# Unused tiles between the pools of a two-MLP kernel: moving operands begin 64 to 256 bytes off the weights' place in a 512-byte row

## The chip, the cores and the metric

The kernel runs on one core of one Trainium2 chip. The metric is device time in microseconds (us) of one execution; less is better. Engines are named as the profile names them: PE is TensorE's matmuls, PEld its weight loads, DVE is VectorE, ACT is ScalarE, POOL is GpSimd, SP the engine that issues the transfers.

## What is computed

Causal retention over 4 batches of 576 tokens with 8 heads of 64, then two MLPs over the 2304 x 512 result, all in float32:

```python
ret = scores * Dmat[None, :, :, :]          # Dmat: gamma_h ** (i - j) for i >= j, else 0
attn = np.matmul(ret, v)
x = attn.transpose(0, 2, 1, 3).reshape(2304, 512)
h = np.maximum(x @ moe_w_in, 0.0)           # 512 -> 2048
x = (h * h) @ moe_w_out                     # 2048 -> 512
h = x @ moe2_w_in
g = h * np.clip(h + 3.0, 0.0, 6.0) / 6.0
return g @ moe2_w_out
```

## The kernel before

**Stages.** The 2304 tokens go through retention and the first MLP in five blocks of 512 or 384 tokens, `BLOCKS`, whose x lies in turn in two tiles, "xa" and "xb". Within a block the loop goes over 16 slices of 128 hidden units. For each, `h_part` (line 612) multiplies a slice of w_in with x (12 matmuls at line 624), ScalarE and VectorE turn the result into g, and `a_part` (line 646) multiplies a slice of w_out with g (12 matmuls at line 661) into four accumulators. Retention of later chunks of 128 tokens stands between these slices, with many matmuls of 64 columns (lines 409 to 497); the first four chunks come ahead of all (lines 277 to 329). While the blocks run, the weights of the second MLP are split and stored for later. The second MLP then runs over three supers of 768 tokens with seven products where a 2 x 2 block product has eight: 112 groups of matmuls with x at line 1185, then as many with the split activations at line 1239.

**Operands.** A float32 number is kept as a high part and a low rest, both of type float32r; each product is made of three matmuls (high with high, high with low, low with high). A matmul has 128 x 128 weights, 512 bytes in each partition, loaded ahead of it, and a moving operand of 512 or 384 columns. Every matmul has its own load. The order of all work is written out by hand; for the second MLP a small clock in the program, `now`, says where the other engines' work is put into the order.

**Where tiles lie.** Tiles come out of pools, and the pools form two stacks in each partition's memory: "left" ones grow up from its bottom, "right" ones down from its top. On the left lie small tiles (`cpool`, `tmpp`), then `gpool` (two g tiles), `xapool` (x of a block of 512), `whi` (weights of slices 8 to 15). On the right lie an unused tile of 320 bytes, "align" (line 107), `upool`, `wlo` (weights of slices 0 to 7), `xbpool` (x of a block of 384) and `apool` (retention). For the second MLP the right stack down to `upool` is taken away (line 1016) and `p1a` put there: its operands of x, `xop` (line 792), six of seven slots of the weights' ring (`ring_load`, line 938), and `spl`, the split activations (`a_cast`, line 1105). When the first MLP is over, the left stack goes as well (line 1040), and `p1c` takes its place with the seventh ring slot and the activations. Sizes are nearly all multiples of 512 bytes. With the 320 bytes of "align" all weights and all moving operands of both MLPs begin 160 bytes into a 512-byte row of the partition's memory, on both stacks.

```python
    pool(ctx, "align", 1, side="right").tile([P, 80], F32, tag="align", name="align")
    upool = pool(ctx, "upool", 1, side="right")
    wlo = pool(right, "wlo", 1, side="right")
    xbpool = pool(right, "xbpool", 1, side="right")
```

## Time and profile before

| | |
|---|---|
| median of 3 runs | 809.81 us (809.74 to 810.19) |
| the profiled execution | 810.17 us |
| its span, first to last instruction | 808.4 us |
| PE busy | 798.3 us, 99% |
| PEld busy | 743.8 us, 92% |
| DVE busy | 604.0 us, 75% |
| ACT busy | 397.0 us, 49% |
| POOL busy | 172.8 us, 21% |
| share of 16 transfer engines' time, queue 1 | 74.5% |
| mean granted clock of TensorE | 0.999 |

The span is the time from the first to the last instruction of one profiled execution; the 1.8 us between it and that execution's own time lie around it. An engine's busy time counts its records' time, a matmul's from its start to a modelled end, so that records of matmuls that follow each other overlap; the step from start to start is read from stretches of the chain, their length divided by their count.

### The profile page before, as it was taken

The page shows a single profiled execution, that of the slowest core. Times are in us where ns is not written, and L with a number is a line of the kernel's source. Part 1 is how long each engine was busy: PE and PEld are TensorE (multiplying, and loading weights), DVE is VectorE, ACT ScalarE, POOL GpSimd, SP SyncE. Part 2 cuts the span into 40 slices and gives each one's busy share as a digit, 9 for nine tenths or more (in the row PEclk, how much of TensorE's full clock was granted, in tenths as well). Part 3 has the DMA queues.
Part 4 walks back from the last instruction along what each step waited for, and adds up shares of the span by engine and source line. Part 5 has one row for each costly group of instructions (what it writes and reads, how often), then busy time and mean ns, then how long its engine had stood idle before and what let it go on. Part 6 is the DMA issues. An engine that isn't in the chain of part 4 may idle for free.

```text
span 808.4 us, 15632 instructions
## 1 busy us (share of the span) xinstructions
PE 798.3 (99%) x5876; PEld 743.8 (92%) x5876; DVE 604.0 (75%) x1106; ACT 397.0 (49%) x736; POOL 172.8 (21%) x163
## 2 busy tenths in 40 slices
PE   8999999999999999999999999999999999999997
PEld 7788889999888899998888999999999999999997
DVE  5989887878755577865557876989677987678764
ACT  1697745444443444444445543666234664335552
POOL 4512230211011011100000056500165300355300
PEclk9999999999999999999999999999999999999999
DMA  9956626777746478766458887979987979977785
GB/s 331 348 191 242 223 92 202 230 220 223 215 145 200 122 246 225 214 175 190 122 162 257 260 295 247 342 269 284 272 257 261 346 253 283 278 258 261 261 235 142
DMA packets 181899, 189.59 MB, mean 235 GB/s; under 512 B 60608, under 2 KB 135488, under 8 KB 181824
## 3 DMA queue, kind: packets, MB, share of 16 engines
q1 hardware_dynamic: 181824, 188.60, 74.5%
q8 instruction: 46, 0.75, 0.4%
q14 instruction: 29, 0.24, 0.1%
HBM read 149.76 MB, written 38.80 MB: 233 GB/s over the span
## 4 chain that ended last, share of the span: by engine, by line
PE 96%; DMA 1%; POOL 1%; issue 0%; SPq 0%; DVE 0%; ACT 0%; DVEq 0%; POOLq 0%
PE acc L661 25%; PE h L624 24%; PE z L1185 22%; PE z L1239 21%; PE at L497 2%; DMA kv<-kv_dram 1%; POOL w L176 0%; PE alone L497 0%; PE sc L409 0%; PE sc L277 0%; PE o L293 0%; POOL raw L141 0%; PE o L460 0%; PE sc L420 0%; DMA out_dram<-t 0%
## 5 line engine op out<-in xcount | busy, mean ns | idle before, releaser
L661 PE MATMUL acc<-g,w 128*128 128x512 f32 (+1 forms) x960 | 212.9, 370 | 0.7 <-ACT g L637 0.4
L624 PE MATMUL h<-x,w 128*128 128x512 f32 (+2 forms) x972 | 210.6, 365 | 0.0
L661 PEld LDWEIGHTS acc<-g,w 128*128 128x128 f32 x960 | 173.8, 188 | 24.9 <-ACT g L637 0.8
L624 PEld LDWEIGHTS h<-x,w 128*128 128x128 f32 x972 | 175.7, 188 | 22.5 <-ACT w L169 0.3
L1185 PE MATMUL z<-xop,ring 128*128 128x384 f32 x1008 | 175.2, 334 | 0.0
L1239 PE MATMUL z<-spl,ring 128*128 128x384 f32 x1008 | 175.2, 334 | 0.0
L1185 PEld LDWEIGHTS z<-xop,ring 128*128 128x128 f32 x1008 | 174.8, 188 | 0.1
L1239 PEld LDWEIGHTS z<-spl,ring 128*128 128x128 f32 x1008 | 174.8, 188 | 0.0
L1100 POOL TENSOR_TENSOR aop<-aop,aop 128x384 f32<-128x384 f32 x96 | 107.5, 1130 | 296.7 <-DVE aop L1097 293.0
L1114 DVE TENSOR_TENSOR spl<-aop,spl 128x384 fp32r<-128x384 f32 x168 | 98.0, 610 | 22.8 <-ACT spl L1110 22.2
L1110 ACT ACTIVATE spl<-aop 128x384 fp32r<-128x384 f32 x168 | 86.0, 523 | 54.7 <-PE z L1239 51.0
L633 ACT ACTIVATE r<-h 128x512 f32<-128x512 f32 (+1 forms) x80 | 44.4, 554 | 112.8 <-PE h L624 112.8
L1094 ACT ACTIVATE aop<-held,small 128x384 f32<-128x384 f32 x72 | 44.4, 617 | 108.3 <-DVE held L1060 107.8
L635 DVE TENSOR_TENSOR r<-r,h 128x512 f32<-128x512 f32 (+1 forms) x80 | 50.5, 631 | 52.7 <-ACT r L633 51.9
L1060 DVE TENSOR_TENSOR held<-z,held 128x384 f32<-128x384 f32 x120 | 66.4, 554 | 26.3 <-PE z L1185 24.1
L637 ACT ACTIVATE g<-r 128x512 fp32r<-128x512 f32 (+1 forms) x80 | 47.2, 590 | 63.3 <-DVE r L635 63.3
L643 DVE TENSOR_TENSOR g<-r,g 128x512 fp32r<-128x512 f32 (+1 forms) x80 | 53.3, 667 | 20.9 <-ACT g L637 18.5
L1097 DVE SCALAR_TENSOR_TENSOR aop<-aop,held 128x384 f32<-128x384 f32 x72 | 49.9, 694 | 17.8 <-ACT aop L1094 16.1
L394 POOL TENSOR_TENSOR qs<-qs,con 128x512 f32<-128x512 f32 x11 | 15.0, 1363 | 134.8 <-DMA qs<-qk_dram 123.0
L751 ACT ACTIVATE uhi<-seven 128x896 fp32r<-128x896 f32 x32 | 30.6, 955 | 23.2 <-DVE seven L741 13.5
L756 DVE TENSOR_TENSOR seven<-seven,uhi 128x896 fp32r<-128x896 f32 x32 | 34.9, 1090 | 7.7 <-ACT uhi L751 7.2
L176 POOL TENSOR_TENSOR w<-wt,w 128x512 fp32r<-128x512 f32 x17 | 22.9, 1347 | 60.2 <-ACT w L169 58.8
(113 smaller groups left out, 628.5 us busy)
## 6 DMA issues: line engine op xcount, KB each, us to landing
ring<-w_out_hl SPq DMA_DIRECT2D x84, 512.0 KB, 4.9
ring<-w_in_hl SPq DMA_DIRECT2D x72, 512.0 KB, 4.8
raw<-w_dram SPq DMA_DIRECT2D x32, 512.0 KB, 7.0
uraw<-w_dram SPq DMA_DIRECT2D x64, 256.0 KB, 3.3
q<-qk_dram SPq DMA_DIRECT2D x17, 512.0 KB, 5.4
w_in_hl<-uhi SPq DMA_DIRECT2D x16, 448.0 KB, 3.6
w_in_hl<-seven SPq DMA_DIRECT2D x16, 448.0 KB, 4.6
w_out_hl<-uhi SPq DMA_DIRECT2D x16, 448.0 KB, 3.2
```

What stands on the lines that cost most here:

```text
L624: nc.tensor.matmul(hp[:, ts], w[:, wi, c * P : (c + 1) * P], x[:, xi, c, ts], start=k == 0, stop=k == 3 * NC - 1,)
L635: nc.vector.tensor_tensor(r, r, hp[:, :nb], ALU.mult)
L637: nc.scalar.activation(g[:, 0, :nb], r, AF.Copy)
L643: nc.vector.tensor_tensor(g[:, 1, :nb], r, g[:, 0, :nb].bitcast(F32), ALU.subtract)
L661: nc.tensor.matmul(acc[d][:, :nb], wt, g[:, gi, :nb], start=first, stop=stop)
L1060: fn(*a)
L1097: stt(f32(q, j), f32(q, j), 6.0, h, ALU.min, ALU.mult)
L1100: nc.gpsimd.tensor_tensor(f32(o, j), f32(a, j), f32(b, j), op)
L1110: act(t[:, 0, :], f32(q, k), AF.Copy)
L1114: tt(t[:, 1, :], f32(q, k), t[:, 0, :].bitcast(F32), ALU.subtract)
L1185: nc.tensor.matmul(bank[q], w[:, wi, u * P : (u + 1) * P], x[:, u, xi, :], start=k == 0 and q not in (2, 4, 3), stop=k == 5, skip_group_ch ...
L1239: nc.tensor.matmul(z[A_BANKS[q][n]][:, :HALF], w[:, k % 2, wi, P * n : P * (n + 1)], sp[:, g, :], start=k == 0 and m == 0 and q not in (2, ...
```

## The change

Between the pools, tiles are allocated that nothing reads or writes, by a new helper `shift`. On the left: 128 bytes below `gpool`, 128 more below `xapool`, 256 more below `whi`, 512 in all. On the right: the 320 bytes of "align" stay, now through the helper, and 256 bytes stand between `wlo` and `xbpool`. In `p1a` a tile of 64 bytes stands between the operands of x and the ring, and another between the ring and what follows it. Built, the places of the operands in a 512-byte row are these:

| matmuls | moving operand | weights |
|---|---|---|
| line 624, h<-x,w | x: 160 before, 416 now | 160, 160 |
| line 661, acc<-g,w | g: 160 before, 288 now | 160, 160 |
| line 1185, z<-xop,ring | xop: 160 before, 32 now | ring: 160 before, 96 now; slot 6: 160, 160 |
| line 1239, z<-spl,ring | spl: 160, 160 | the same ring |

The instructions and their order are those of before on every engine. Of the waits one stands elsewhere: on POOL, the second of the first four operations of line 1100 waits for a count of ScalarE that the third of them waited for before.

```diff
+    def shift(stack, name, size, side):
+
+        pool(stack, name, 1, side=side).tile([P, size // 4], F32, tag=name, name=name)
+
+    shift(left, "shift_g", 128, "left")
     gpool = pool(left, "gpool", 2, side="left")
+    shift(left, "shift_xa", 128, "left")
     xapool = pool(left, "xapool", 1, side="left")
+    shift(left, "shift_whi", 256, "left")
     whi = pool(left, "whi", 1, side="left")
-
-    pool(ctx, "align", 1, side="right").tile([P, 80], F32, tag="align", name="align")
+    shift(ctx, "align", 320, "right")
     upool = pool(ctx, "upool", 1, side="right")
     wlo = pool(right, "wlo", 1, side="right")
+    shift(right, "shift_xb", 256, "right")
     xbpool = pool(right, "xbpool", 1, side="right")
...
             for st in x_first:
                 do(st[0])
+            p1a.tile([P, 16], F32, tag="shift_ring", name="shift_ring")
...
     p1c = pool(ctx, "p1c", 1, side="left")
+    p1a.tile([P, 16], F32, tag="shift_spl", name="shift_spl")
```

## Rows read from the trace of the kernel before

**Rows 1.** The page, part 1: busy us (share of span) x instructions.
```profile
PE 798.3 (99%) x5876; PEld 743.8 (92%) x5876; DVE 604.0 (75%) x1106; ACT 397.0 (49%) x736; POOL 172.8 (21%) x163
```
**Rows 2.** The page, part 4: the chain's shares by engine.
```profile
PE 96%; DMA 1%; POOL 1%; issue 0%; SPq 0%; DVE 0%; ACT 0%; DVEq 0%; POOLq 0%
```
**Rows 3.** Waits of PE: us in total, times, longest us.
```profile
PE sc L277 <- DVE q L265: 1.0, 1, 1.0
PE unread L852 <- POOL early L846: 1.0, 1, 1.0
...
PE acc L661 <- ACT g L637: 0.4, 1, 0.4
PE acc L661 <- POOL w L176: 0.3, 1, 0.3
```
**Rows 4.** The chain in the first MLP: start us, us, what.
```profile
33.49 2.72 PE h L624 x12
36.21 2.72 PE acc L661 x12
...
126.07 2.08 PE acc L661 x12
128.15 2.08 PE h L624 x12
```
**Rows 5.** The chain in the second MLP.
```profile
453.33 58.26 PE z L1185 x336
511.60 58.24 PE z L1239 x336
569.84 58.24 PE z L1185 x336
628.08 58.24 PE z L1239 x336
686.32 58.24 PE z L1185 x336
744.55 56.17 PE z L1239 x324
800.73 0.02 issue
```
**Rows 6.** Busy time in stretches: engines' us (x), granted clock, transfer share, GB/s.
```profile
core 0: us, PE busy (x) PEld busy (x) DVE busy (x) ACT busy (x) POOL busy (x), PEclk, DMA share, GB/s
126.07:138.69 12.62, 12.62 (x173) 12.30 (x173) 9.40 (x22) 5.74 (x11) 0.10 (x1) 1.00 0.68 213
453.33:511.59 58.26, 58.26 (x338) 58.26 (x337) 44.54 (x77) 23.50 (x46) 29.37 (x28) 1.00 0.85 280
511.60:569.80 58.20, 58.20 (x337) 58.20 (x337) 50.17 (x96) 34.58 (x72) 6.38 (x4) 1.00 0.90 296
628.10:686.30 58.20, 58.20 (x337) 58.20 (x337) 49.54 (x95) 34.48 (x71) 6.38 (x4) 1.00 0.92 297
```
**Rows 7.** PE's groups by shape: xcount | busy us, mean ns | idle before.
```profile
L1185 PE MATMUL z<-xop,ring 128*128 128x384 f32 x1008 | 175.2, 334 | 0.0
L1239 PE MATMUL z<-spl,ring 128*128 128x384 f32 x1008 | 175.2, 334 | 0.0
L661 PE MATMUL acc<-g,w 128*128 128x512 f32 x576 | 140.3, 392 | 0.7 <-ACT g L637 0.4 <-POOL w L176 0.3
L624 PE MATMUL h<-x,w 128*128 128x512 f32 x564 | 135.8, 390 | 0.0
L661 PE MATMUL acc<-g,w 128*128 128x384 f32 x384 | 72.7, 337 | 0.0
L624 PE MATMUL h<-x,w 128*128 128x384 f32 x384 | 71.8, 334 | 0.0
...
L624 PE MATMUL h<-x,w 128*128 128x256 f32 x24 | 3.1, 286 | 0.0
```
**Rows 8.** POOL's first operations of line 1100 in the timeline.
```profile
463.13 4.38 POOL L1100 TENSOR_TENSOR aop<-aop,aop 128x384 f32<-128x384 f32 x4 [112.54 <-DVE aop L1097]
```
**Rows 9.** Line 303: one group in PE's timeline; durations min/median/max of all.
```profile
15.41 1.16 PE L303 MATMUL o<-q,states 128*128 128x128 f32 x8
...
L303 PE MATMUL o<-q,states x24: 275/275/377, 15.4 to 22.8; 128*128 128x128 f32 x24
```
**Rows 10.** PEld's groups by shape: weight loads of 128 and 64 columns.
```profile
L1185 PEld LDWEIGHTS z<-xop,ring 128*128 128x128 f32 x1008 | 174.8, 188 | 0.1
...
L497 PEld LDWEIGHTS alone<-p,v 64*64 64x64 f32 x176 | 6.0, 135 | 0.0
```

## The prediction

> **What bounds the kernel now.** I read the page's first part, then the chain that ended last, then TensorE's groups with their shapes, and last single stretches of the chain and of engine time. The first part says that TensorE is the bound: 798.3 of 808.4 us busy, VectorE next with 604.0 [rows 1]. The chain says that nothing else matters: 96% of the span is TensorE, the transfer named next has 1% [rows 2]. Its waits are a few, the longest 1.0 us, all in the start or of that size [rows 3]. So a matmul's step, the time from one start to the next, times the number of matmuls is the kernel.

> The step can be read from stretches of the chain in which TensorE does one thing. Twelve matmuls of 512 columns take 2.72 us, 226.7 ns each; twelve of 384 take 2.08 us, 173.3 ns [rows 4]. In the second MLP 336 of 384 columns take 58.26 or 58.24 us, 173.4 and 173.3 ns [rows 5]. [...] Every matmul thus costs its columns and **32 more, 13.3 ns**, whatever its length and whichever of the four kinds it is. There are 564 + 384 + 24 of the kind h<-x,w, 576 + 384 of acc<-g,w, 1008 of z<-xop,ring and 1008 of z<-spl,ring [rows 7], 3948 in all. Their excess is 3948 x 13.3 = 52.6 us, 6.5% of the span, and that is all this change can get at.

> **The change, part by part.** It adds tiles that nobody writes or reads. No instruction is added, removed or moved on any engine, no transfer changes its size or its pieces; what remains is where tiles lie. I cost four parts.

> The waits. One differs: on POOL the first subtraction of line 1100 waits for a ScalarE count that the second one waited for before. POOL had stood idle 112.54 us before these operations, for VectorE [rows 8], and the ScalarE count lies in the first MLP, long over. Cost 0, and the cover is that idle time; without it the worst would be one operation of about 1.1 us (4.38 us for four) on an engine that no part of the chain between 453.33 and 800.73 us goes through [rows 5, 8].

> VectorE, ScalarE and POOL operations on moved tiles. Each goes over the same elements at another place. They have room: in the second MLP VectorE is busy 50.17 of 58.20 us, ScalarE 34.58 [rows 6]. If each VectorE operation there became a tenth longer, VectorE would still fit (55.2 us). Cost 0.

> Transfers into and out of moved tiles. The ring's pieces land 64 bytes off their former place. In the second MLP the transfer engines are at 0.85 to 0.92 of their time [rows 6], so this is the tightest cover; TensorE would begin to wait if the transfers there got some 9% slower (1/0.92). Nothing in their size or number changes, and I put 0.

> TensorE's own reads, the only term that may be large. In the kernel before, each moving operand of the four kinds begins at the same place of a 512-byte row as its weights, so **the trace shows no step at another distance** between them; the cost has to be bounded. The bound below is the whole excess: 0 columns more instead of 32 gives -52.6 us. The nearest row with a smaller excess is line 303, weights of the same 128 columns, where eight short matmuls take 1.16 us with a last one of 377 ns [rows 9]: (1.16 - 0.377)/7 = 111.9 ns a step. Those steps are paced by the weight loads. A load of 128 columns takes 188 ns and one of 64 takes 135 [rows 10], so 64 columns more are 53 ns, a column is 0.83 ns, and 128 are 106 ns; what is left over is 5.9 ns. If the large matmuls fell to 5.9 ns, they would gain 13.3 - 5.9 = 7.4 ns each, 29.2 us. The bound above is as open: should moving operand and weights stand best as they are, and each load cost the stream as much again, it is +13.3 ns a matmul, +52.6 us.

> Between these ends I take **0**, for two reasons from the rows. First, the two streams do not keep step. Weights are read at 0.83 ns a column [rows 10], the moving operand at 0.417 ns (2.4 per ns). While one 512-byte row of weights is read, the moving operand runs through two rows of its own, so it passes every place of a row twice, and a shift of 64, 128 or 256 bytes changes when the two meet, not how often. Second, the step does not heed other readers: it is the same to 0.1 ns between a stretch with VectorE at 44.54, ScalarE at 23.50 and POOL at 29.37 us busy and one with 50.17, 34.58 and 6.38, with transfers at 0.85 and 0.90 [rows 5, 6]. Those engines go through rows at all places. If meeting at a place cost TensorE a cycle, the steps would scatter with them.

> [...]

> **The sum** is 0 on the profiled execution, which took 810.17 us for a span of 808.4. That is 0.36 above the median of the runs shown, 809.81, so I forecast 809.8; the likeliest case alone lies within 809.0 and 810.6.

> **The rivals.**

> Faster: the excess is the two reads in each other's way, and it is there because they share their place. For it: the excess is the same in all four kinds and at 256, 384 and 512 columns, and in all of them the distance is 0, just the case that the change ends. A cost that comes once for each weight load and not with the columns is what a collision with that load would look like. Against it: the two rates above, and that the slow steps of line 303 also have distance 0 with an excess of only 5.9 ns. Time: 809.8 - 29.2 = 780.6 if all four kinds fall to 5.9 ns; the first MLP alone has 1932 matmuls, 14.3 us, so 795.5, and the second 2016, 14.9 us, so 794.9. One kind's shift may help and another's not, since they are 256, 128 and 64. The far edge is 757.2.

> [...]

> Slower: distance 0 is the good case. The moving operand runs at twice the weights' pace, so from one common start they part at once and meet again only as the load ends; from any other distance they meet in the middle of the load, and the stream is held there. For it: the step is the same to the column in all kinds, as if nothing collided now, and the first steps of the program show that loads alone can set the pace. Against it: the second reason above. Price: if one kind of about 1000 matmuls is held for as much as the excess is now, 1008 x 13.3 = 13.4 us, 823.2; all kinds, 862.4. It decides from 0.4 ns a step on (1.6 us / 3948), one column.

> That the change does not do what it says is a small rival. The built program has x at 416 and g at 288 bytes into a row, the first MLP's weights at 160; xop at 32 and the ring at 96, spl at 160. But ring slot 6 of 7 lies in the other pool and stays at 160: for a seventh of the second MLP the distances are 128 (xop) and 0 (spl). A gain or loss in that kind would be short by a seventh, 144 of 1008; it changes no sign.

> **How the numbers follow.** This kernel can be told from no change at about 0.2%, 1.6 us, so "same" is 808.2 to 811.4. I give no effect **0.44**: two reasons from rows, but neither from a step at another distance. Faster gets **0.32**, since the excess is real, constant, and belongs to the weight load. Slower gets **0.24**. Faster splits into 0.28 above 766 us and 0.04 below, where less than 2.2 of the 13.3 ns would be left, which no row with 128-column weights shows. Slower splits into 0.08 up to 823 us, one kind held, and 0.16 beyond. The range from 766 to 823 us holds 0.28 + 0.44 + 0.08 = 0.80. It is wide because cases of both signs hold more than half of the chance.

> **What would show it.** In the changed kernel's chain, the stretches of twelve should read 2.72 us (512 columns) and 2.08 us (384), and the four long stretches of the second MLP 58.2 us, each a direct measure of one distance: 256 in the lines h<-x,w, 128 in acc<-g,w, 64 in the second MLP's two. The faster rival shows as 2.63 us for twelve of 512 columns and 55.7 us for 336; the slower one as a stretch longer than today's in one kind, 2.88 us or 62.7 us at the price given. If the chain's stretches stand and the time moves all the same, it is a wait, and TensorE's waits of a few tenths to 1.0 us [rows 3] would have company on lines 1185 or 1239 from transfers. What would make the prediction wrong is any step that differs by more than 0.4 ns from 226.7 or 173.3.

## The result and the profile after

The changed kernel takes 816.63 us (816.37 to 816.87, 3 runs) against 809.81: a ratio of 1.0077, with an interval of 1.0063 to 1.0091. It is slower by 6.8 us. The forecast of no effect was wrong; the time lies in the range given for all cases, on the side of the slower rival.

The page of the changed kernel, parts 1 and 3, beside [rows 1]:

```profile
PE 805.8 (99%) x5876; PEld 748.3 (92%) x5876; DVE 603.7 (74%) x1106; ACT 396.8 (49%) x736; POOL 173.6 (21%) x163
...
q1 hardware_dynamic: 181824, 188.60, 74.4%
```

The number of instructions on each engine and the number of packets are the same. TensorE's matmuls are busy 7.5 us longer and its loads 4.5, where the span grew by 6.7 (815.1 against 808.4); no other engine moved by more than 0.8. The chain, with lines 8 to 10 higher than before, says where. Its stretches in the first MLP answer to [rows 4], those in the second to [rows 5] (start us, us, what):

```profile
137.53 2.12 PE acc L669 x12
139.65 2.08 PE h L632 x12
...
217.61 2.79 PE acc L669 x12
220.40 2.73 PE h L632 x12
...
457.52 58.91 PE z L1195 x336
516.43 58.34 PE z L1249 x336
574.78 59.00 PE z L1195 x336
633.78 58.34 PE z L1249 x336
692.13 59.00 PE z L1195 x336
751.12 56.28 PE z L1249 x324
807.40 0.02 issue
```

The rows read so. With g, 128 bytes off, twelve matmuls of 512 columns went from 2.72 to 2.79 us and of 384 from 2.08 to 2.12; with x, 256 off, they stayed within 0.01. The second MLP begins at 457.52 instead of 453.33, so the first gave away 4.2 us. From there to the last matmul it is 807.40 - 457.52 = 349.88 us, where it was 800.73 - 453.33 = 347.40 [rows 5]: 2.5 us more, of which the three stretches with xop have 0.65 + 0.76 + 0.76 = 2.2 and those with spl 0.3. 4.2 + 2.5 is the whole 6.7. It is no wait; TensorE's longest ones in the changed kernel answer to [rows 3] and are as small:

```profile
PE unread L860 <- POOL early L854: 1.0, 1, 1.0
PE o L301 <- POOL kv L277: 0.8, 1, 0.8
PE h L632 <- POOL w L184: 0.7, 1, 0.7
```

So the step of the matmuls itself has changed, in some kinds and not in others.

### The profile page after: what moved, and what is told of

It is laid out like the page before. It is cut to its first block, busy times and chain, and to the rows that moved or that the text cites. A ratio compares the mean times of both kernels' runs of the same rounds, so it can differ in the third digit from the quotient of the medians.

```text
span 815.1 us, 15632 instructions
## 1 busy us (share of the span) xinstructions
PE 805.8 (99%) x5876; PEld 748.3 (92%) x5876; DVE 603.7 (74%) x1106; ACT 396.8 (49%) x736; POOL 173.6 (21%) x163
## 4 chain that ended last, share of the span: by engine, by line
PE 95%; DMA 2%; DVE 1%; SPq 1%; POOL 1%; ACT 0%; issue 0%; DVEq 0%; POOLq 0%
PE acc L669 24%; PE h L632 24%; PE z L1195 22%; PE z L1249 21%; PE at L505 2%; DMA kv<-kv_dram 1%; PE alone L505 0%; DVE wt L169 0%; PE sc L417 0%; POOL raw L149 0%; PE o L468 0%; PE sc L428 0%; POOL w L184 0%; POOL states L357 0%; DMA out_dram<-t 0%
## 5 line engine op out<-in xcount | busy, mean ns | idle before, releaser
L669 PE MATMUL acc<-g,w 128*128 128x512 f32 (+1 forms) x960 | 216.5, 374 | 0.0
L632 PEld LDWEIGHTS h<-x,w 128*128 128x128 f32 x972 | 176.0, 188 | 24.5 <-POOL w L184 0.9
L1195 PE MATMUL z<-xop,ring 128*128 128x384 f32 x1008 | 177.4, 337 | 0.0
L1195 PEld LDWEIGHTS z<-xop,ring 128*128 128x128 f32 x1008 | 177.0, 187 | 0.1
L759 ACT ACTIVATE uhi<-seven 128x896 fp32r<-128x896 f32 x32 | 30.5, 955 | 23.2 <-DVE seven L749 13.4
```

Of the source, the lines that this page charges most:

```text
L632: nc.tensor.matmul(hp[:, ts], w[:, wi, c * P : (c + 1) * P], x[:, xi, c, ts], start=k == 0, stop=k == 3 * NC - 1,)
L669: nc.tensor.matmul(acc[d][:, :nb], wt, g[:, gi, :nb], start=first, stop=stop)
L1195: nc.tensor.matmul(bank[q], w[:, wi, u * P : (u + 1) * P], x[:, u, xi, :], start=k == 0 and q not in (2, 4, 3), stop=k == 5, skip_group_ch ...
```

## The experiments

All are the kernel before with unused tiles of other sizes; each computes the whole result. In the traces of all of them each engine has the instructions of before in the same order. Distance means: place of the moving operand in a 512-byte row less that of its weights; 448 and -64, say, are the same distance. Diffs stand against the changed kernel and show only tiles that differ; where a tile's line is taken out and none put in, the run leaves the tile out. Lines of the code stand 10 to 13 higher in these runs than in the kernel before. The first four were run together and share their runs of the kernel before (809.99 us).

**g alone.**

```diff
-    shift(left, "shift_xa", 128, "left")
+    shift(left, "shift_xa", 384, "left")
-    shift(left, "shift_whi", 256, "left")
-    shift(right, "shift_xb", 256, "right")
-            p1a.tile([P, 16], F32, tag="shift_ring", name="shift_ring")
-    p1a.tile([P, 16], F32, tag="shift_spl", name="shift_spl")
```

> Only g is moved, to 128 bytes past its weights (g at 288 in a 512-byte row, all else at 160). Theory D (the distance between moving operand and weights in a 512-byte row sets the step; 128 and -64 are bad, 0, 64 and 256 are as good as each other): twelve acc matmuls of 512 columns take 2.79 us as in the changed kernel, against 2.72, of 384 columns 2.12 against 2.08; 48 x 0.07 + 32 x 0.04 = 4.6 us at most, and the first MLP ended 4.2 us later in the changed kernel; so 813.5 to 814.4 us. Theory A (the moving operand's own place in a row sets the step, 160 and 416 good, 32 and 288 bad): the same here. Theory W (a wait or a transfer that the new places delay, not the step of the matmuls): 809.8 us and 2.72 us for twelve.

Measured: 814.48 us, ratio 1.0053 (1.0038 to 1.0068). The chain of this run:

```profile
152.16 2.12 PE acc L671 x12
154.27 2.08 PE h L634 x12
...
217.42 2.79 PE acc L671 x12
220.21 2.73 PE h L634 x12
...
457.35 58.24 PE z L1195 x336
515.59 58.24 PE z L1249 x336
```

Only acc is long, and the second MLP, back at distance 0, is back at 58.24. The loss of the first MLP belongs to g's 128 bytes. Theory W falls.

**xop alone.** Against the changed kernel all shifts but `align` and `shift_ring` are taken out; xop is then at -64, in all seven slots of the ring alike.

```diff
-    shift(left, "shift_g", 128, "left")
-    shift(left, "shift_xa", 128, "left")
-    shift(left, "shift_whi", 256, "left")
-    shift(right, "shift_xb", 256, "right")
-    p1a.tile([P, 16], F32, tag="shift_spl", name="shift_spl")
```

> Only xop is moved, 64 bytes short of the ring (xop at 96, ring and all else at 160). Theory D: a long stretch of 336 matmuls with xop takes 58.95 us as in the changed kernel, against 58.25, the stretches with spl stay at 58.24; three stretches, 3 x 0.7 = 2.1 us, so 811.9 us. Theory A says nothing of 96, a place not seen so far: 809.8 if it counts with 160, 811.9 if with 32. Theory W: 809.8 us, or a stretch that is longer because of a wait that the trace names.

Measured: 810.86 us, ratio 1.0011 (1.0001 to 1.0020): 0.9 us above before, where theory D had 2.1. The chain says why, with one longer stretch of 0.45 us instead of three:

```profile
453.21 58.69 PE z L1196 x336
511.90 58.24 PE z L1250 x336
570.14 58.24 PE z L1196 x336
628.38 58.25 PE z L1250 x336
686.63 58.24 PE z L1196 x336
```

One distance, one kind of matmul, the same 336 of them, and two values: 58.69 us (174.7 ns a step) when xop follows the first MLP, 58.24 (173.3) when it follows spl. At one distance the step thus had more than one mean here, each lasting through a stretch of 336 matmuls. In the trace of the changed kernel the starts of the single matmuls with xop, at the same distance, show two patterns with these means: its first stretch begins with steps of 173, 173, 174 ns, again and again, its third with steps like 173, 178, 171, 177, 174. That what went before decides between them is the likeliest reading, from this one trace. From this came theory L of the later expectations.

**x and spl alone**, the parts of the change that looked harmless; slot 6 of the ring is moved along.

```diff
-    shift(left, "shift_g", 128, "left")
-    shift(left, "shift_xa", 128, "left")
+    shift(left, "shift_xa", 256, "left")
-            p1a.tile([P, 16], F32, tag="shift_ring", name="shift_ring")
+    p1c.tile([P, 112], F32, tag="shift_p1c", name="shift_p1c")
```

> What of the change should be harmless: x 256 bytes off its weights and spl 64 past the ring, g and xop at their weights' place (xop and ring both at 96). Theory D: within 0.2% of before, 809.4 to 810.6 us, h stretches of 2.72 and 2.08 us, spl stretches of 58.24, xop stretches of 58.25. Theory A: xop at 96 may show as longer xop stretches if that place is bad. A third theory J (each change of distance from one group of matmuls to the next costs some matmuls' steps): about 25 ns at each of 160 changes between h and acc, up to 4 us, 813 us.

Measured: 810.27 us, ratio 1.0004 (0.9995 to 1.0014).

```profile
215.81 2.72 PE acc L671 x12
218.53 2.72 PE h L634 x12
...
453.00 58.26 PE z L1197 x336
511.27 58.24 PE z L1251 x336
```

Theory D holds; xop at 96, with its ring there too, is as good as at 160, and the change of distance at each group, 256 for h and 0 for acc, costs nothing. Theory J, which had up to 813 us, falls.

**Everything 128 bytes on.** g, x, xop, spl and all weights at 288, distance 0.

```diff
-    shift(left, "shift_xa", 128, "left")
-    shift(left, "shift_whi", 256, "left")
-    shift(ctx, "align", 320, "right")
+    shift(ctx, "align", 192, "right")
-    shift(right, "shift_xb", 256, "right")
-            p1a.tile([P, 16], F32, tag="shift_ring", name="shift_ring")
-    p1a.tile([P, 16], F32, tag="shift_spl", name="shift_spl")
+    p1c.tile([P, 32], F32, tag="shift_p1c", name="shift_p1c")
```

> Moving operands and weights of both MLPs all 128 bytes further on, at 288 in a 512-byte row: the distance is 0 everywhere as before. Theory D: 809.8 us and every stretch as before. Theory A: g, x, xop and spl are all at a bad place; acc and h stretches of 2.79 and 2.12 us, 336 matmuls in 58.95: 2 x 4.2 + 6 x 0.7 = 12.6 us, 822 us.

Measured: 810.20 us, ratio 1.0003 (0.9993 to 1.0012), with stretches of 2.72, 2.08 and 58.24 us (58.27 the first).

```profile
215.57 2.72 PE acc L671 x12
...
569.32 58.24 PE z L1196 x336
```

The operand's own place does nothing here: theory A, which would have had 822, falls. The distance is what counts.

**The change with slot 6 moved too**, so that no distance jumps within a stretch of the second MLP.

```diff
+    p1c.tile([P, 112], F32, tag="shift_p1c", name="shift_p1c")
```

> The whole change, and ring slot 6 moved to the ring's place as well (448 bytes ahead of it in its pool), so that in the second MLP all seven slots stand at one distance: -64 to xop, 64 to spl. Theory L (lock: matmuls and loads that follow each other at one distance fall into a steady pattern; a jump of the distance costs about 25 ns and can leave them in a longer pattern, which lasts until the next jump): the xop stretches of 336 matmuls are each 58.24 us, or 58.7 us all through, and no longer 58.9 to 59.0, and the spl stretches 58.24 instead of 58.34; the second MLP gets 0.9 to 2.4 us shorter, 814.2 to 815.8 us in all. Theory D (each distance has its step): xop stays at 58.9, only spl gains, 3 x 0.1 us; 816.3 us.

Measured: 815.61 us (before beside it 810.74; ratio 1.0059, 1.0042 to 1.0076).

```profile
457.33 59.36 PE z L1198 x336
516.70 58.24 PE z L1252 x336
574.94 58.69 PE z L1198 x336
633.62 58.24 PE z L1252 x336
691.86 58.69 PE z L1198 x336
```

With spl the jumps to slot 6 were all there was: 58.34 is 58.24 without them. With xop at -64 the mixed values of 58.91 to 59.00 have become pure ones, a third mean step among them: 59.36 is 176.7 ns. The total lies in theory L's range, but 59.36 us is a value that neither theory had for a stretch with xop. The trace of the changed kernel bears the mixture out: its first stretch with xop runs at a mean of 173.3 ns for some 60 matmuls, past the first passage of slot 6 at 174.7, past the second and the third at 176.7 and past the fourth at 174.7; the pattern changes at these passages and not between them. But the places of what ran before do not decide alone: up to the first passage the two kernels do the same at the same places, and this one has 176.7 ns from the start, where the changed kernel has 173.3. So a single value of a stretch with xop may be in part chance; the sum of the three with xop came out within 0.2 us (176.74 us against 176.91).

**128 bytes for other kinds.** x at 128 and g at 0; ring, with slot 6, 128 below both xop and spl.

```diff
-    shift(left, "shift_g", 128, "left")
-    shift(left, "shift_whi", 256, "left")
+    shift(left, "shift_whi", 384, "left")
-    shift(right, "shift_xb", 256, "right")
+    shift(right, "shift_xb", 384, "right")
-            p1a.tile([P, 16], F32, tag="shift_ring", name="shift_ring")
+            p1a.tile([P, 96], F32, tag="shift_ring", name="shift_ring")
+    p1c.tile([P, 96], F32, tag="shift_p1c", name="shift_p1c")
-    p1a.tile([P, 16], F32, tag="shift_spl", name="shift_spl")
+    p1a.tile([P, 32], F32, tag="shift_spl", name="shift_spl")
```

> 128 bytes for other operands: x at 128 past its weights, g at its weights' place; in the second MLP xop and spl both 128 past the ring, all seven slots alike. Theory D: h groups of twelve take 2.79 and 2.12 us, acc groups 2.72 and 2.08; the six long stretches 58.9 us each; 809.8 + 4.4 + 6 x 0.7 = 818.4 us. Theory L: in the second MLP the distance never jumps, so stretches settle at 58.24 us, the first perhaps at 58.7; in the first MLP h or acc groups may be long, since the distance jumps at each. 810 to 815 us.

Measured: 818.94 us, one run, with 810.74 for the kernel before beside it.

```profile
217.59 2.73 PE acc L671 x12
220.32 2.79 PE h L634 x12
...
457.69 58.98 PE z L1198 x336
516.67 58.99 PE z L1252 x336
```

The long groups have moved from acc to h with the 128 bytes. In the second MLP the moving operands stand where they did before and the weights have moved; it costs 0.75 us a stretch, with xop and with spl alike, without a jump. At 128 no stretch settles at 58.24: theory D, with 818.4 us, is right there. Whether the moving operand or the weights are shifted makes no difference that shows, and h pays for 128 what acc paid.

**x and g both at 128; xop and spl at -128**, no jumps in either MLP.

```diff
-    shift(left, "shift_xa", 128, "left")
-    shift(left, "shift_whi", 256, "left")
+    shift(left, "shift_whi", 384, "left")
-    shift(right, "shift_xb", 256, "right")
+    shift(right, "shift_xb", 384, "right")
```

with 128 bytes ahead of the ring, 384 behind it and 128 for slot 6.

> x and g both 128 past their weights, so that nothing jumps between h and acc; in the second MLP all at -128. Theory D: h and acc groups both long, 2.79 and 2.12 us, and the six stretches at 58.9 or more: 809.8 + 9 + 4 = 823 us. Theory L: without jumps the groups settle at 2.72 and 2.08 us but for those after retention, and the stretches at 58.24: 810 to 812 us.

Measured: 822.73 us, one run.

```profile
218.76 2.79 PE acc L671 x12
221.56 2.79 PE h L634 x12
...
460.56 59.14 PE z L1198 x336
```

h and acc are both at 2.79, the stretches of 336 at 59.13 or 59.14 us. Theory D's 823; theory L had 810 to 812 and falls for these two distances.

**Five more pairs of distances**, made in the same way with other sizes (the first MLP's distance is that of x and g, the second's that of xop and spl, all slots alike). One run each, beside 810.74 us for the kernel before in the first and 809.95 in the others; the lines under each are from its chain. The first of them, without its tiles in `p1a` and `p1c`:

```diff
-    shift(left, "shift_g", 128, "left")
+    shift(left, "shift_g", 192, "left")
-    shift(left, "shift_xa", 128, "left")
-    shift(left, "shift_whi", 256, "left")
+    shift(left, "shift_whi", 320, "left")
-    shift(right, "shift_xb", 256, "right")
+    shift(right, "shift_xb", 320, "right")
```

> Distances not seen so far: x and g 192 past their weights, xop and spl 320 past the ring, no jumps within an MLP. Theory L: 2.72 and 2.08 us, 58.24 us, 810 us, or a longer pattern all through one MLP. Theory D: each of the two numbers is its own; nothing is said but that h and acc, and xop and spl, are alike. If a distance had less than the 32 columns of excess, it would show here as under 2.72 or 58.24 us.

Measured: 816.16 us.

```profile
152.76 2.08 PE acc L671 x12
...
215.10 2.80 PE h L634 x12
...
459.37 58.24 PE z L1198 x336
```

The two lengths part here: at 192 matmuls of 512 columns are long and those of 384 are not. Then -32 and 32:

> Distance -32 in the first MLP, 32 in the second. Theory D (each distance has its step, for each number of columns): if a small distance is like 0, all as before, 2.72, 2.08 and 58.24 us, 810 us; if what counts is that moving operand and load don't share 64 bytes, as 64 is good and 128 bad, nothing is said of 32. Theory L keeps only -64: nothing longer here than the jump's 25 ns. A step below 2.72 or 58.24 us at any distance would be a gain on both kernels.

Measured: 822.60 us.

```profile
152.53 2.08 PE acc L671 x12
...
217.68 2.80 PE acc L671 x12
...
518.47 59.36 PE z L1252 x336
```

A small distance is not like 0: theory D's 810 us, for the case that it is, is missed by 12.6 us, and so is theory L's "nothing longer". 320 and 192:

> Distance 320 (-192) in the first MLP, 192 in the second. The run before had 192 at 2.80 us for 512 columns and 2.08 for 384, and 320 at 58.24 us for 336 of 384. Theory D with the columns: 384 columns stay at 2.08 in the first MLP and 58.24 in the second; for 512 columns 320 is bad like 192 if a distance and its negative are alike, 2.80 us, 815 us; if they are not, 2.72 us and 810 us.

Measured: 814.56 us.

```profile
151.74 2.08 PE acc L671 x12
...
216.59 2.75 PE acc L671 x12
...
513.76 58.69 PE z L1252 x336
```

The 815 us came near by luck: twelve of 512 columns took 2.75 us and not 2.80, and the second MLP, for which 58.24 was said, took 58.69. 64 and 256:

> Distance 64 in the first MLP, 256 in the second. Theory D: 256 is good for 384 columns in the changed kernel's h groups, so 58.24 us in all six stretches; 64 is good for 384 columns with spl, so 2.08 us; for 512 columns it is open: 2.72 us and 810 us if like 0, 2.79 and 816 us if like 128.

Measured: 811.26 us.

```profile
151.10 2.08 PE acc L671 x12
...
215.95 2.75 PE acc L671 x12
...
512.68 58.24 PE z L1252 x336
```

384 columns came as theory D had them; 512 columns at 64 are like neither 0 nor 128. -64 in both:

> Distance -64 everywhere. In the second MLP nothing jumps: theory L (at -64 several patterns can last, 173.3, 174.7 or 176.7 ns a step, and the entry decides) expects each stretch at 58.24, 58.69 or 59.36 us, and the same value in all, since neither entry nor distance changes between them; theory D as one value, between 58.24 and 58.9. In the first MLP, groups of 384 columns at 2.08 to 2.12 us; for 512 columns open.

Measured: 823.35 us.

```profile
153.23 2.08 PE acc L671 x12
...
218.37 2.80 PE acc L671 x12
...
519.20 59.36 PE z L1252 x336
```

All stretches of 336 are at 59.36, one value throughout, as theory L had it; theory D had less.

Put together, in us:

| distance | 12 of 512 columns | 12 of 384, first MLP | 336 of 384, second MLP |
|---|---|---|---|
| 0 | 2.72 | 2.08 | 58.24 |
| 32 | | | 59.36 |
| 64 | 2.75 | 2.08 | 58.24 |
| 128 | 2.79 | 2.12 | 58.99 |
| 192 | 2.80 | 2.08 | 58.69 |
| 256 | 2.72 | 2.08 | 58.24 |
| 320 (-192) | 2.75 | 2.08 | 58.24 |
| 384 (-128) | | | 59.14 |
| 448 (-64) | 2.80 | 2.08 | 58.24, 58.69 or 59.36 |
| 480 (-32) | 2.80 | 2.08 | |

Many of these distances were seen in one trace only. For 512 columns distances that differ by 256 agree: 0 and 256, 64 and 320, 192 and 448. The least is 2.72, 2.08 and 58.24, at 0 and 256; no stretch goes below it. No version here beats the kernel before. Of the theories D is left, with a mean step for each distance and each number of columns, but for 384 columns at -64 and 192, where one distance had more than one mean; only there do patterns that last, as in theory L, show.

## Why the prediction failed, point by point

**The bound** was read rightly: TensorE's step times its count is the kernel, and the loss is in the step. The 13.3 ns follow from the two steps of [rows 4]: 226.7 - 173.3 = 53.4 ns for 128 columns more are 0.417 ns a column, 2.4 columns per ns; 512 columns take 213.3 ns of the 226.7, 384 take 160.0 of the 173.3, and 13.3 ns, 32 columns' worth, are left in both.

**The waits, the other engines' operations and the transfers** cost what was put for them, 0. The first operations of line 1110 on POOL still wait for VectorE, now after 113.92 us of idle time, and TensorE has no wait for any of these in the second MLP.

**TensorE's own reads** is the step that failed. The prediction took 0 between -52.6 and +52.6 us; the runs show +6.8 for this change. In the traces it is 4.2 in the first MLP, with g at 128, and in the second 2.2 with xop and 0.3 with spl. The first reason given was that the two streams run at 0.83 and 0.417 ns a column, the author's estimates from [rows 10] and the steps of [rows 4], so that a shift moves the time at which they meet and not how often. When they meet no trace shows, and the rates do not give the cost: weights of 128 columns with a moving operand of 512 took 2.72 us a dozen at distance 0 and 2.79 or 2.80 at 128, 192, -64 and -32. The second reason, that the step does not heed VectorE, ScalarE, POOL and the transfers, stands for the stretches seen (with xop alone moved, one with VectorE busy 42.81, ScalarE 22.53 and POOL 29.52 us and the transfers at 0.85 took 58.24 us, like one with 50.17, 34.58, 6.38 and 0.90 in [rows 5, 6]), but it is about other engines and was carried over to TensorE's two reads, of which it says nothing.

In these runs the step depends on where the two operands lie to each other: g alone, moved by 128 bytes, costs 5.8 ns a matmul of 512 columns (232.5 against 226.7). What in the chip makes the distance count no run here tells, nor, as all weights of a stretch lie at one place, whether it is the matmul's own load or a neighbour's. The cause is shown as far as the distance, and open behind it.

**The slower rival** had the sign and, in part, the size. It priced one kind held by 13.3 ns a matmul, 823.2 us; measured were 5.8 ns for 512 columns and about 3 for 384 (2.12 against 2.08 us) with g, and 2.2 ns with xop (2.17 us over 1008 matmuls). Its mechanism falls in one point: it held that from any other distance than 0 the streams meet in the middle of the load. 256 is free for both lengths (2.72 and 2.08 us a dozen), and 64 and 320 for 384 columns (2.08 us a dozen, 58.24 us for 336).

**The faster rival** has nothing left at the distances tried, ten in all: no group of twelve and no stretch of 336 has a mean step under 226.7 ns for 512 columns or 173.3 for 384. At none of them did the place of the operands end the 13.3 ns of excess, of which the lower edge of the range, 766 us, left 2.2; what they are stays open.

**The small rival**, slot 6, was mis-stated: "short by a seventh" took distances to act matmul by matmul. With spl, where 0 and 64 are both free, the jump from one to the other cost 0.1 us a stretch, four passages of slot 6 at some 25 ns. With xop it threw the matmuls from one lasting pattern into another (in the first stretch from a mean of 173.3 ns to 174.7 and on to 176.7); slot 6's own distance of -128, at 59.14 us for 336, accounts for about 0.13 us a stretch (48 matmuls), and the patterns for the rest.

## What to carry to other kernels

## What the runs showed that was not expected

The mean steps of long stretches come in a few values: for 384 columns 173.3, 174.7, 175.6, 176.0 and 176.7 ns, for 512 columns 226.7, 229.2, 232.5 and 233.3. A single step need not be one of these values: by the starts in the traces, matmuls of 512 columns follow each other in 226 or 227 ns at distance 0, before the change, but after it, with g at 128, in 229 and 237 or 238 by turns through most of a group of twelve. What a bad distance does in these two traces is thus a repeating pattern of shorter and longer steps, and its mean is the price. At -64, the same matmuls at the same distance ran at three of them (58.24, 58.69 and 59.36 us for 336), each through a whole stretch; they differ in what ran before, but not always in its places (the first stretch with xop began at 173.3 ns in the changed kernel and at 176.7 with slot 6 moved), and what decides was not found. So a short test of one distance can show a value that another neighbourhood does not: 384 columns at 192 ran at 2.08 us a dozen in the first MLP and at 174.7 ns, not 173.3, in the second, and at -64 at 2.08 us against 176.7 ns. Why these values and not others, and why for 512 columns distances 256 bytes apart agreed in the three pairs tried (2.72, 2.75 and 2.80 us a dozen), was not found.
